# Routing's operations queue behind x's normalisation, turned rows are copied before shifted ones, and the first block's weights are asked for in eight pieces

## The chip, the cores and the metric

The kernel runs on one core of one Trainium2 chip. Its time is the device time of one execution in microseconds (us); a measurement is the median of several. The profile is of one execution, and positions in it are counted from its first instruction.

## What is computed

Sliding-window causal attention over 8 sequences of 576 tokens with 8 heads of 64 features, and behind it a layer of 8 experts in which every token goes to one expert. A local gate decides whether a token takes the expert of its own logits or that of the token before it, so the choice runs as a chain along the sequence.

```python
scores = q @ k.T / sqrt(64)                  # only 0 <= pos_q - pos_k < 64
attn_out = softmax(scores) @ v               # (8, 8, 576, 64) -> x (8, 576, 512)
logits = x @ w_gate                          # 8 experts
local_gate = sigmoid(x @ w_local)
for b in range(B):
    prev_e = -1
    for s in range(S):
        fresh_e = argmax(logits[b, s])
        e = fresh_e if s == 0 or local_gate[b, s] < 0.5 else (prev_e if prev_e >= 0 else fresh_e)
        prev_e = e
        h = maximum(x[b, s] @ w1[e], 0)      # 512 -> 1024
        out[b, s] = softmax(logits[b, s])[e] * (h @ w2[e])
```

## The kernel before

The 4608 tokens are cut into nine stages (`sc`) of 512; in every stage four pairs of heads (`hp`) are worked on, which makes 36 units, written (sc, hp). `attention` runs over the units in this order. For unit i it first issues the scores of unit i + 2 (`scores`: TensorE products, ScalarE exponentials, and on VectorE the multiplication with a mask, L421; for the units in `BIASED`, among them all of stage 6, the mask is added on TensorE instead), then the values of unit i (`values`: 64 small TensorE products, then on VectorE the reciprocal of the sums, L436, for later stages the gate columns, L439, and x's normalisation, L441). The output of the values lies in one of two PSUM buffers (`pair`), used in turns, so the values of a unit wait until the normalisation of the unit two before has read its buffer.

TensorE, ScalarE and SyncE (SP, which issues most DMAs) run in the order of the program (`manual_schedule`). VectorE and GpSimd (POOL) are queues in order too, but a scheduler that works on estimated times puts them together, and it may place an operation that is ready by its estimate ahead of others that the program issues earlier. `issue_after(ins)` adds an order at compile time: what is issued under it on the engine of `ins` comes behind `ins` in the queue.

Between a stage's first units `shift(sc + 1)` copies the rows of v half a tile further, into `vb` of the next stage: ScalarE does L360, L363 and L367, POOL L361 and L365; two of its parts are taken per unit. For stages 0 to 3 the gate logits come from turned rows: `turn` transposes x on TensorE into one of the two PSUM buffers and ScalarE copies the result out (L305); its second half is done at head pair 0 of the next stage. For the later stages (`GATED`) the gate columns ride along with v; `gates` and `spread` make them, by way of the single PSUM bank of `bank`, and ScalarE copies them out (L346 to L348).

`Router.first` finds, from the logits of the first 3 1/2 stages, which tokens fill the first three expert blocks. It is a generator whose parts are issued between the units by `step`, which runs once ahead of the values of a unit and once behind them. Every call takes 0.8 (`HALF`) off `pause`; once `pause` is not above zero the next part is issued, and `pause` becomes its weight plus what was left (not below -0.8). A part is yielded with its weight and with whether the part behind it begins with a PSUM operation; such a part isn't issued in a step called with `free` false. `free` is false at the first step of head pair 3 and at the second of head pair 2 when the next stage is in `GATED`. The parts are `gate` (maxima, two transposes with scans on VectorE behind them, L812 and L822, the carry, L833, the experts, L845, counts, L858, ranks), then `experts_of` and the places (`pl`, `places`), then `table`: comparisons that make one-hot rows (`rowh`, L957) and columns, a product of these (L980), and from it the row indices (`idx1`, `gx1`, L984 to L989). With `gx1` POOL gathers the first block's rows (`Experts.rows`, L1162). `weigh` stores the routing weights.

Two steps are marked in SP's queue for the first block's weights: at unit (6, 3) w1 and at (7, 1) w2 are asked for, each in four pieces of 512 KB at once, behind a tiny DMA (`until`) that makes SP wait for that unit's reciprocals. Then come the expert blocks (`Experts.run`): the first turns its gathered rows on TensorE (L1196, copied by ScalarE, L1197), computes `hidden` (L1414) and, on the way, VectorE's sums of w2 (L1231). SP's next weights wait for gathered rows of the second block (`held`). A second pass of the router (`Router.second`) is interleaved with the first blocks.

Of the kernel before, what the change touches and what calls it, by code (L numbers as in the profile page):

```python
# [8 lines left out]
F32 = mybir.dt.float32  # L9
# [10 lines left out]
P = 128  # L20
# [147 lines left out]
def attention(ctx, tc, ring, kq, v3, v4, vt, vh, xs, lt, ok, wg, wg2, ident, rt, ex):  # L168
# [65 lines left out]

    late = cp.tile([1, 4], F32, name="late")

# [187 lines left out]
    def values(sc, hp, p, x, g):  # L424
        va, vb, n = vas[sc], vbs[sc], width(sc)
        xo = pair()
        for s in range(4):
            for j in range(2):
                for par, w in enumerate((vb, va)):
                    b = 2 * s + par  # L430
                    nc.tensor.matmul(xo[par * WIN:(par + 1) * WIN, j, s * VW:s * VW + n],  # L431
                                     lhsT=p[:, j, b * WIN:(b + 1) * WIN], rhs=w[:, s, 2 * hp + j, :n],
                                     start=True, stop=True)
        o = xo[:, :, :4 * VW].rearrange("p j (c x) -> p j c x", x=VW)
        r = allr[:, sc, hp]
        nc.vector.reciprocal(r, o[:, :, :, DH])  # L436
# [4 lines left out]
        nc.vector.tensor_tensor(x[:, :, hp].rearrange("p c j d -> p j c d"), o[:, :, :, :DH],  # L441
                                rr.to_broadcast([P, 2, 4, DH]), op=Alu.mult)

# [27 lines left out]
    for i, (sc, hp) in enumerate(units):  # L471
# [230 lines left out]
class Router:  # L702
# [9 lines left out]
    def __init__(self, ctx, tc, lt, xs, tabs, ident):  # L712
        self.nc, self.lt, self.xs, self.tabs, self.ident = tc.nc, lt, xs, tabs, ident
        self.pool = ctx.enter_context(tc.tile_pool(name="rt", bufs=1))
        self.tc, self.behind, self.links = tc, None, []
# [58 lines left out]
    def gate(self, part, psum):  # L774
# [170 lines left out]
    def table(self, psum, cs, ns, lo, hi, idx, gx):  # L945
# [5 lines left out]
        for k in range(0, len(pieces), 2):  # L951
            built = []
            for b, m in pieces[k:k + 2]:
                rowh = self.oh_p.tile([P, PIECE, P], BF16, name="rowh")[:, :m]
                if ns == FIRST:
                    sh = [P, m, P]
                    vec.tensor_tensor(rowh, self.io128.to_broadcast(sh), last(lo[:, b:b + m]).to_broadcast(sh),  # L957
                                      op=Alu.is_equal)
                    yield 0.15 * m, False
                one = self.oh_p.tile([P, PIECE, ns], BF16, name="one")[:, :m]  # L960
# [33 lines left out]
    def first(self, psum):  # L994
# [20 lines left out]
        vec.tensor_tensor(pl, rank, mid(self.lim1).to_broadcast(CE), op=Alu.is_ge)  # L1015
        vec.scalar_tensor_tensor(pl, pl, float(2 * N), rank, Alu.mult, Alu.add)
        yield 1.2, False
        vec.tensor_tensor(pl, pl, mid(foff).to_broadcast(CE), op=Alu.add)
        vec.tensor_tensor(pl, pl, self.oh[:, :C1], op=Alu.mult)
        lo, hi = self.places(pl, C1)  # L1020

        vec.tensor_tensor(rank, rank, mid(self.lim1).to_broadcast(CE), op=Alu.subtract)
        yield 2.5, False
        self.weigh(0)
        yield from self.table(psum, slice(0, C1), FIRST, lo, hi, tabs["idx1"], tabs["gx1"])

    def second(self, psum):
# [72 lines left out]
        vec.tensor_tensor(pl, pl, plh, op=Alu.add)  # L1100
        vec.tensor_scalar(none, self.rank[:, :C1], 0.0, float(2 * N), Alu.is_lt, Alu.mult)
        vec.tensor_tensor(pl[:, :C1], pl[:, :C1], none, op=Alu.add)
# [28 lines left out]
class Experts:  # L1131
# [38 lines left out]
    def weights(self, st, n, names=("w1", "w2"), behind=lambda: None):  # L1170
        ej, at = (self.tabs["ej1"], -1 - n) if n < 0 else (self.tabs["ej"], n)
        e = self.nc.values_load(ej[0:1, at:at + 1], engines=[ET.SP], min_val=0, max_val=E - 1,
                                skip_runtime_bounds_check_because="a count of experts, at most E - 1")
        behind()
        for name, w, a, b in (("w1", self.w1, DK, F), ("w2", self.w2, FK, D)):
            if name not in names:
# [6 lines left out]
            st[name] = t.rearrange("p (a b) -> p a b", a=a)  # L1183
        return st

    def begin(self):
# [432 lines left out]
```

## Time and profile before

| | |
|---|---|
| median of 3 runs | 642.59 us (640.96 to 642.63) |
| the profiled execution, its own time | 642.1 us |
| its span, first to last instruction | 640.0 us |
| mean granted TensorE clock | 0.994 |
| instructions | 14994 |
| attention stage, to the first block's matmuls | 0 to 133.4 us |
| HBM traffic | 259 GB/s over the span |

How such a profile is read: PE is TensorE (PEld its weight loads, which overlap), DVE VectorE, ACT ScalarE, POOL GpSimd, SP SyncE's DMA queue. A row of the timeline has start, duration, engine, line, operation, output and inputs, and in brackets how long the engine sat idle before it and what released it. A row of waits has engine, tile and line, the releaser, and the total, number and longest of the waits. "issue" is time for which the profile shows no wait. An engine's idle time matters only where that engine sets the end.

### The profile page before, as it was taken

What the parts mean: (1) busy time and instruction counts of PE and PEld (TensorE: products, weight loads), DVE (VectorE), ACT (ScalarE), POOL (GpSimd) and SP (SyncE); (2) the same over time, 40 slices, a digit from 0 to 9 for tenths busy, and PEclk for the clock granted to TensorE, in tenths of its full rate; (3) what the DMA queues carried; (4) which work ended last, traced back from release to release, by engine and by line L of the source; (5) the groups of instructions that cost most, each with busy time, mean ns of one, the idle gap of its engine ahead of it and who ended that gap; (6) DMA issues with size and microseconds to landing.
All of it is one profiled execution on the core that took longest, in us unless ns stands there. A gap on an engine that the chain in (4) does not pass through costs nothing. (4 is left out here: it accounts for less than half of the span.)

```text
span 640.0 us, 14994 instructions
## 1 busy us (share of the span) xinstructions
PE 615.6 (96%) x6367; PEld 544.2 (85%) x6367; DVE 402.3 (63%) x752; ACT 200.6 (31%) x368; POOL 133.1 (21%) x132
## 2 busy tenths in 40 slices
PE   8889998899999999999999999999999999999995
PEld 7777777788889999978997999887997998899994
DVE  6676588879968775273654683362917752886730
ACT  3766765612572122113120312021211221213120
POOL 5422112430103202120302120211312022111101
PEclk9999998999999999999999999999999999999998
DMA  9999996969757645786958665769768556956501
GB/s 338 416 418 406 385 366 241 348 236 337 237 171 246 244 166 198 242 316 236 387 189 291 218 234 212 259 235 367 263 228 324 185 199 232 379 167 225 209 17 38
DMA packets 29318, 166.43 MB, mean 260 GB/s; under 512 B 8451, under 2 KB 9497, under 8 KB 20026
## 3 DMA queue, kind: packets, MB, share of 16 engines
q1 hardware_dynamic: 20394, 135.54, 58.4%
q0 software_dynamic: 8848, 29.85, 12.2%
q8 instruction: 52, 0.85, 0.5%
q14 instruction: 24, 0.20, 0.1%
HBM read 146.18 MB, written 19.59 MB: 259 GB/s over the span
## 5 line engine op out<-in xcount | busy, mean ns | idle before, releaser
L1394 POOL DMA_INDIRECT out_dram<-y,idx x36 | 41.1, 1141 | 339.1 <-DVE y L1327 196.5
L1318 PE MATMUL hp<-ws,hs 128*128 128x256 f32 x384 | 88.7, 380 | 0.0
L1318 PEld LDWEIGHTS hp<-ws,hs 128*128 128x128 f32 x384 | 72.6, 190 | 10.5 <-issue 0.8
L1268 PE MATMUL hp<-xs,ws 128*128 128x128 f32 x672 | 79.6, 275 | 0.0
L1268 PEld LDWEIGHTS hp<-xs,ws 128*128 128x128 f32 x672 | 77.3, 192 | 0.0
L1327 DVE SCALAR_TENSOR_TENSOR y<-hp,xg,kept 128x256 f32<-128x256 f32 x48 | 22.6, 482 | 74.2 <-issue 47.0
L1414 PE MATMUL hp<-xt,w 128*64 128x64 f32 (+2 forms) x640 | 66.2, 276 | 0.0
L1414 PEld LDWEIGHTS hp<-xt,w 128*128 128x128 f32 (+1 forms) x640 | 60.8, 170 | 4.1 <-issue 0.7
L1318 PE MATMUL hp<-w,h 128*128 128x256 f32 x256 | 61.1, 382 | 0.0
L1162 POOL DMA_INDIRECT xg<-xs,gx x40 | 50.3, 1258 | 45.6 <-issue 37.4
L1279 DVE TENSOR_TENSOR h<-hp,keep 128x512 f32<-128x512 f32 x42 | 28.6, 690 | 48.1 <-PE hp L1268 48.0
L1268 PEld LDWEIGHTS hp<-xt,w 128*128 128x128 f32 x448 | 53.2, 192 | 2.7 <-issue 1.3
L1268 PE MATMUL hp<-xt,w 128*128 128x128 f32 x448 | 54.7, 275 | 0.0
L1318 PEld LDWEIGHTS hp<-w,h 128*128 128x128 f32 x256 | 47.2, 190 | 6.3 <-issue 0.4
L431 PE MATMUL xo<-vb,p 128*64 128x74 f32 (+1 forms) x576 | 44.5, 230 | 7.0 <-issue 2.9
L416 ACT ACTIVATE p<-sp 128x512 f32<-128x512 f32 x72 | 39.2, 595 | 38.0 <-PE sp L385 35.9
L385 PEld LDWEIGHTS sp<-w 64*64 64x64 f32 x1296 | 38.7, 138 | 12.1 <-issue 8.5
L421 DVE TENSOR_TENSOR p<-p,mask 128x1024 f32<-128x1024 f32 x29 | 36.1, 1245 | 19.5 <-ACT p L416 19.3
L431 PEld LDWEIGHTS xo<-vb,p 128*64 128x64 f32 x576 | 38.9, 138 | 9.9 <-issue 4.4
L385 PE MATMUL sp<-w 64*64 64x128 f32 (+1 forms) x1296 | 43.8, 270 | 2.6 <-issue 1.5
L431 PE MATMUL xo<-va,p 128*64 128x74 f32 (+1 forms) x576 | 44.5, 230 | 1.2 <-issue 1.2
L1280 ACT ACTIVATE h<-h 128x512 f32<-128x512 f32 x42 | 26.3, 630 | 59.1 <-DVE h L1279 59.1
(280 smaller groups left out, 955.0 us busy)
## 6 DMA issues: line engine op xcount, KB each, us to landing
w<-in_w_dram SPq DMA_DIRECT2D x42, 2048.0 KB, 9.2
w<-in_kq_dram SPq DMA_DIRECT2D x17, 1024.0 KB, 8.7
w<-in_w_dram SPq DMA_DIRECT2D x24, 512.0 KB, 9.3
xs<-x POOLq DMA_DIRECT2D x9, 1024.0 KB, 9.5
va<-in_v_dram SPq DMA_DIRECT2D x5, 1184.0 KB, 8.9
vtt<-in_vt_dram SPq DMA_DIRECT2D x5, 1024.0 KB, 7.2
va<-in_v_dram SPq DMA_DIRECT2D x3, 1040.0 KB, 12.2
va<-in_v_dram SPq DMA_DIRECT2D x2, 520.0 KB, 6.8
```

The source lines that it names most:

```text
L385: nc.tensor.matmul(sp[j][c * WIN:(c + 1) * WIN, a:b], lhsT=kt[h, hp, block * WIN:(block + 1) * WIN], rhs=qt[h, hp, a:b], start=not biased, ...
L416: nc.scalar.activation(p[:, j], sp[j], Act.Exp, scale=DH ** -0.5)
L421: masked.append(nc.vector.tensor_tensor(p, p, m.to_broadcast([P, 2, SC]), op=Alu.mult))
L431: nc.tensor.matmul(xo[par * WIN:(par + 1) * WIN, j, s * VW:s * VW + n], lhsT=p[:, j, b * WIN:(b + 1) * WIN], rhs=w[:, s, 2 * hp + j, :n], ...
L1162: asked = self.nc.gpsimd.indirect_dma_start(out=x, out_offset=None, in_=self.xs[:rows, :], in_offset=bass.IndirectOffsetOnAxis(ap=gx[:, s: ...
L1268: nc.tensor.matmul(out[:, m, :], lhsT=a[:, kk, m * P:(m + 1) * P], rhs=b[:, kk, :], start=start and m + kk == 0, stop=stop and (m, kk) == ...
L1279: nc.vector.tensor_tensor(o, x, y, op=add)
L1280: nc.scalar.activation(o, x if y is None else o, Act.Relu)
L1318: nc.tensor.matmul(out, lhsT=a[:, m, :], rhs=b[:, m, :], start=start and m == 0, stop=stop and m == FK // 2 - 1, skip_group_check=True)
L1327: nc.vector.scalar_tensor_tensor(y[i][:, j * w:(j + 1) * w], x, pw[i], y2, Alu.mult, Alu.add)
L1394: self.nc.gpsimd.indirect_dma_start(out=self.out[:, :], out_offset=bass.IndirectOffsetOnAxis(ap=st["idx"][:, s:s + 1], axis=0), in_=y, in_ ...
L1414: nc.tensor.matmul(hp[a, i, :], lhsT=st["w1"][:, kk, m * P:(m + 1) * P][:, a], rhs=st["xt"][:, kk, :n], start=(kk == 0), stop=(kk == DK - 1))
```

## The change

- `Router.after()` gives an `issue_after` on x's last issued normalisation (`rt.norm`, set in `values`). Under it are now issued: the rows `rowh` of the first table, which are also made in halves of five chunks with a part each; `experts_of`, the steps of `pl`, `places` and the rank's subtraction in `first`, cut into three parts in place of two; and in `second` the operation that makes `none`.
- The part with the scans in `gate` has the weight 2.4 in place of 1.5 in the first pass.
- The second step of a unit is not free at head pairs 2 and 3 (before: 2 alone) when the next stage is in `GATED`.
- At head pair 0 of stages 1 to 4 the two parts of `shift` are issued behind `turn`, not ahead of it.
- w1 of the first block is asked for in single pieces at (6, 3), (7, 0), (7, 1) and (7, 2), w2 at (8, 0) to (8, 3), each behind its own `until`.

```diff
-    late = cp.tile([1, 4], F32, name="late")
+    late = cp.tile([1, 3 + 2 * HP], F32, name="late")
...
-        nc.vector.tensor_tensor(x[:, :, hp].rearrange("p c j d -> p j c d"), o[:, :, :, :DH],
-                                rr.to_broadcast([P, 2, 4, DH]), op=Alu.mult)
+        rt.norm = nc.vector.tensor_tensor(x[:, :, hp].rearrange("p c j d -> p j c d"), o[:, :, :, :DH],
+                                          rr.to_broadcast([P, 2, 4, DH]), op=Alu.mult)
...
-        for _ in range(2 if sc else 4):
-            next(moves, None) if moves else None
+        late_moves = hp == 0 and sc and sc - 1 not in GATED
+
+        def move():
+            for _ in range(2 if sc else 4):
+                next(moves, None) if moves else None
+
+        if not late_moves:
+            move()
...
+        if late_moves:
+            move()
...
-            ex.jobs = [ex.weights({}, -1, ("w1",), lambda: until(2, allr[:1, sc, hp, 0, :1]))]
+            ex.jobs = [ex.weights({}, -1, (), lambda: until(2, allr[:1, sc, hp, 0, :1]))]
+            ex.piece(ex.jobs[0], "w1", 0)
...
-        step(not (hp == 2 and sc + 1 in GATED))
-        if (sc, hp) == (NSC - 2, 1):
-            ex.weights(ex.jobs[0], -1, ("w2",), lambda: until(3, allr[:1, sc, hp, 0, :1]))
+        step(not (hp >= 2 and sc + 1 in GATED))
+        at = i - (len(units) - 2 * HP)
+        if 0 <= at < 2 * HP and at != HP - 1:
+            until(3 + at, allr[:1, sc, hp, 0, :1])
+            ex.piece(ex.jobs[0], "w1" if at < HP else "w2", at % HP + (at < HP))
...
+    def after(self):
+
+        return self.tc.issue_after(self.norm.ins) if self.norm else nullcontext()
...
-        yield 1.5, True
+        yield 1.5 if part else 2.4, True
...
-                    vec.tensor_tensor(rowh, self.io128.to_broadcast(sh), last(lo[:, b:b + m]).to_broadcast(sh),
-                                      op=Alu.is_equal)
-                    yield 0.15 * m, False
+                    for c in range(0, m, PIECE // 2):
+                        d = min(c + PIECE // 2, m)
+                        sh = [P, d - c, P]
+                        with self.after():
+                            vec.tensor_tensor(rowh[:, c:d], self.io128.to_broadcast(sh),
+                                              last(lo[:, b + c:b + d]).to_broadcast(sh), op=Alu.is_equal)
+                        yield 0.15 * (d - c), False
...
-        self.experts_of(tabs["ej1"], FB, [(FB, fend)])
...
+        with self.after():
+            self.experts_of(tabs["ej1"], FB, [(FB, fend)])
+            vec.tensor_tensor(pl, rank, mid(self.lim1).to_broadcast(CE), op=Alu.is_ge)
+            vec.scalar_tensor_tensor(pl, pl, float(2 * N), rank, Alu.mult, Alu.add)
         yield 1.2, False
...
+        with self.after():
+            vec.tensor_tensor(pl, pl, mid(foff).to_broadcast(CE), op=Alu.add)
+            vec.tensor_tensor(pl, pl, self.oh[:, :C1], op=Alu.mult)
+        yield 0.8, False
+        with self.after():
+            lo, hi = self.places(pl, C1)
+            vec.tensor_tensor(rank, rank, mid(self.lim1).to_broadcast(CE), op=Alu.subtract)
+        yield 1.7, False
...
+        with self.after():
+            vec.tensor_scalar(none, self.rank[:, :C1], 0.0, float(2 * N), Alu.is_lt, Alu.mult)
...
+    def piece(self, st, name, i):
+        w, a, b = (self.w1, DK, F) if name == "w1" else (self.w2, FK, D)
+        if not i:
+            t = self.ring.tile([P, a * b], F32, name="w")
+            st[name] = t.rearrange("p (a b) -> p a b", a=a)
+        m = a // PARTS
+        src = w[bass.ds(st["e"], 1)].rearrange("o p (a b) -> (o p) a b", a=a)
+        self.nc.sync.dma_start(out=st[name][:, i * m:(i + 1) * m], in_=src[:, i * m:(i + 1) * m])
```

More of the change, by code (lines that the diff above doesn't have):

```diff
@@ L714, in __init__ @@
         self.pool = ctx.enter_context(tc.tile_pool(name="rt", bufs=1))
-        self.tc, self.behind, self.links = tc, None, []
+        self.tc, self.behind, self.links, self.norm = tc, None, [], None
         self.rows_of(ctx, tc, "rt_oh1")
@@ L1014, in first @@
         rank = self.rank[:, :C1]
-        vec.tensor_tensor(pl, rank, mid(self.lim1).to_broadcast(CE), op=Alu.is_ge)
-        vec.scalar_tensor_tensor(pl, pl, float(2 * N), rank, Alu.mult, Alu.add)
+        with self.after():
+            self.experts_of(tabs["ej1"], FB, [(FB, fend)])
+            vec.tensor_tensor(pl, rank, mid(self.lim1).to_broadcast(CE), op=Alu.is_ge)
+            vec.scalar_tensor_tensor(pl, pl, float(2 * N), rank, Alu.mult, Alu.add)
         yield 1.2, False
[L1018 to L1023, printed above, removed]
+        with self.after():
[6 more added lines that the diff above has]
+        yield 1.7, False
         self.weigh(0)
@@ L1100, in second @@
         vec.tensor_tensor(pl, pl, plh, op=Alu.add)
-        vec.tensor_scalar(none, self.rank[:, :C1], 0.0, float(2 * N), Alu.is_lt, Alu.mult)
+        with self.after():
+            vec.tensor_scalar(none, self.rank[:, :C1], 0.0, float(2 * N), Alu.is_lt, Alu.mult)
         vec.tensor_tensor(pl[:, :C1], pl[:, :C1], none, op=Alu.add)
@@ L1174, in weights @@
         behind()
+        st["e"] = e
         for name, w, a, b in (("w1", self.w1, DK, F), ("w2", self.w2, FK, D)):
```

## The prediction, made before the result was known

> **What bounds the kernel now.** I read the engine shares first, then TensorE's own waits, then the stretches around those waits.
>
> ```profile
> span 640.0 us, 14994 instructions
> PE 615.6 (96%) x6367; PEld 544.2 (85%) x6367; DVE 402.3 (63%) x752; ACT 200.6 (31%) x368; POOL 133.1 (21%) x132
> 133.41:626.00 492.59, 491.31 (x3487) 440.95 (x3486) 305.34 (x513) 119.38 (x231) 90.69 (x77) 1.00 0.66 239
> ```
>
> TensorE (PE) is the bound. From 133.41 us, where the first expert block's matmuls begin, to 626 us it idles 1.3 us in 492.6. So the experts are a fixed length behind one point, the start of that block, and only what brings this point forward counts. All removable idle time lies in the attention stage ahead of it. Its waits from 40 us on:
>
> ```profile
> PE xo L431 <- issue: 3.4, 3, 1.8
> PE xo L431 <- DVE x L441: 2.5, 1, 2.5
> PE xo L431 <- ACT p L305: 1.5, 3, 0.8
> PE r L822 <- DVE loc L817: 0.9, 1, 0.9
> PE r L812 <- ACT va L348: 0.6, 1, 0.6
> ```
>
> The second row is the largest single wait: unit (6,1), written (stage, head pair), needs the PSUM buffer that x's normalisation of unit (5,3) has to read out.
>
> ```profile
> 96.28 1.24 DVE L1019 TENSOR_TENSOR pl<-pl,oh 128x112 f32<-128x112 f32 x1
> 97.44 1.18 DVE L1101 TENSOR_SCALAR none<-rank 128x112 f32<-128x112 f32 x1
> 99.66 1.49 DVE L957 TENSOR_TENSOR rowh<-io,lo 128x1280 bf16<-128x1280 f32 x1
> 101.06 0.20 DVE L436 RECIPROCAL allr<-xo 128x8 f32<-128x8 f32 x1
> 101.45 0.68 DVE L441 TENSOR_TENSOR x<-xo,allr 128x512 f32<-128x512 f32 x1
> ```
>
> VectorE (DVE) is a queue in order, and routing operations that the program issues three units later were put ahead of that reciprocal. The wait also costs clock (columns: the stretch, its length, busy time of PE, PEld, DVE, ACT and POOL with counts, granted clock, DMA share, GB/s):
>
> ```profile
> 99.67:102.18 2.51, 0.00 (x0) 0.00 (x0) 2.51 (x7) 2.20 (x4) 0.00 (x0) 1.00 0.65 255
> 102.18:103.98 1.80, 1.80 (x32) 1.65 (x32) 1.80 (x9) 0.00 (x0) 0.75 (x1) 0.63 0.24 89
> 103.98:105.90 1.92, 1.92 (x39) 1.80 (x37) 1.73 (x6) 0.00 (x0) 0.00 (x0) 0.50 1.01 412
> 109.76:110.95 1.19, 1.19 (x34) 1.11 (x33) 0.52 (x1) 1.17 (x4) 0.00 (x0) 1.00 0.50 213
> 113.18:114.23 1.05, 1.05 (x40) 0.98 (x37) 1.03 (x2) 1.03 (x3) 1.05 (x2) 1.00 0.97 102
> ```
>
> After 2.51 us of idling, one unit's values take 1.80 us where 1.19 is usual, and its scores 1.92 where 1.05 is usual: 0.61 + 0.87 = 1.5 us more.
>
> **The change part by part.**
>
> *Routing behind x's normalisation.* The guarded operations (rowh, places, pl, none) can no longer run ahead of the last normalisation issued. The wait of 2.5 us and the slow clock of 1.5 us go: -4.0. In its place nothing is late: with DVE free, (5,3) is normalised while PE does the next scores, 1.05 us or more.
>
> *New weights of the parts and the stricter free.* With 2.4 in place of 1.5, and no PSUM part at the second step of head pair 3, L812 moves from (4,3) to the first step of (5,0) and L822 from there to (5,1). Their waits of 0.6 and 0.9 on the same rows have a unit more to pass: -1.5.
>
> *Turned rows first.* At head pair 0 of stages 2 to 4, the copy L305 leaves ahead of L360 and L363:
>
> ```profile
> 55.04 0.63 ACT L360 COPY vb<-va 64x520 f32<-64x520 f32 x1
> 55.57 1.17 ACT L363 COPY vb<-va 64x1184 f32<-64x1184 f32 x1
> 56.76 1.01 ACT L305 COPY p<-xo 128x1024 f32<-128x1024 f32 x1
> 57.83 0.27 PE L431 MATMUL xo<-vb,p 128*64 128x65 f32 x1 [0.82 <-ACT p L305]
> ```
>
> L305 then ends at about 56.05, ahead of PE, which was ready 0.82 before 57.83. ScalarE's sum of the three copies is unchanged, so the next exponentials start as before; vb is read four units later, so the two delayed copies cost nothing. All three waits go: -1.5. POOL's copies of the same shift keep their order.
>
> Together -7.0, all of it ahead of 107.21 us, where the values of (6,2) end.
>
> *What the steps now do to DVE.* Counting the pause by hand (0.8 off per step, a part's weight added) gives the units in which routing is issued (a: the step ahead of the values, b: behind them):
>
> ```
>           L812  L822  L833  L845  L858  pl    places  rowh  L980
> before    4,3b  5,0a  5,0b  5,1b  5,2a  6,0b  6,1a    6,2b  7,1a
> after     5,0a  5,1a  5,1b  6,0a  6,0b  6,3a  7,0a    7,1a  8,0a
> ```
>
> So L812, issued in 5,0a, leaves a pause of -0.8 + 2.4 = 1.6; it is 0.8 in 5,0b and zero in 5,1a, where L822 goes. Of before, the trace has L980 just ahead of the values of (7,1), at 114.66:
>
> ```profile
> L980 PE MATMUL r<-colh,rowh x14: 168/168/181, 114.2 to 114.6; 128*128 128x12 bf16 x14
> ```
>
> After, L845 finds pause above zero in 5,2a, and then no PSUM part may go until 6,0a. All behind it comes later, L980 by three units, in (8,0). That is DVE's heavy stage. The units of stage 6 take their masks as biases on PE; from (7,0) on each has a mask on DVE again:
>
> ```profile
> 116.75 1.22 DVE L421 TENSOR_TENSOR p<-p,mask 128x1024 f32<-128x1024 f32 x1
> 117.88 0.20 DVE L436 RECIPROCAL allr<-xo 128x8 f32<-128x8 f32 x1
> 118.86 1.22 DVE L421 TENSOR_TENSOR p<-p,mask 128x1024 f32<-128x1024 f32 x1
> ```
>
> From start to start that is 1.1 for a mask and 1.0 for a normalisation. The budget from 107.21 to the first block:
>
> ```profile
> 107.21:124.72 17.51, 16.32 (x415) 13.18 (x415) 14.60 (x31) 11.15 (x21) 6.79 (x5) 1.00 0.89 288
> 124.72:133.41 8.69, 6.94 (x179) 6.37 (x173) 6.17 (x13) 3.24 (x6) 0.81 (x1) 1.00 0.89 347
> ```
>
> PE is busy 23.3 of 26.2 us, DVE 14.60 + 6.17 = 20.8. What moves in is read off the stretches that it fills now:
>
> ```profile
> 94.79:96.28 1.49, 1.49 (x48) 1.33 (x52) 1.42 (x12) 1.44 (x4) 0.14 (x1) 1.00 0.99 335
> 98.54:101.06 2.52, 1.13 (x42) 0.97 (x34) 2.36 (x9) 2.50 (x4) 0.01 (x1) 1.00 0.96 367
> 102.62:103.59 0.97, 0.97 (x23) 0.97 (x21) 0.97 (x5) 0.00 (x0) 0.56 (x1) 0.51 0.10 29
> ```
>
> 1.42 + 2.36 + 0.97, and 0.27 for L1019 without its wait: 5.0 us (a few small operations in these rows stay, a few outside them come; I let them cancel). L1019 itself shows one more cost. It took 1.24 where L1022, of the same size, takes 0.27:
>
> ```profile
> 96.09 0.27 DVE L1022 TENSOR_TENSOR rank<-rank,lim 128x112 f32<-128x112 f32 x1
> 96.14 1.26 POOL L361 COPY vb<-va 64x1184 f32<-64x1184 f32 x1 [11.48 <-PE xo L431]
> ```
>
> It ends as POOL's copy does. Stage 7's two POOL copies now meet the moved operations: nothing at best, 2 x 0.97 at worst; I take 0.65, as DVE reaches them midway. The Trainium skill ("SBUF — State Buffer", Who interferes with whom) speaks against the change here: a DVE operation with two SBUF inputs blocks until a reading GpSimd operation ends. By that rule alone both copies would stop one operation each, and the sum would be 1.3 us worse.
>
> DVE therefore becomes the bound of the last nine units. The last values, (8,3), need the normalisation of (8,1), not that of (8,2): 20.8 - 1.0 + 5.0 + 0.65 + about 1.0 in which it waits for exponentials = 26.4 us after 107.21 (in this scale), then 1.2 of values: 27.6 against 26.2 before.
>
> *The gather of the first block's rows.* gx comes behind L980. DVE's work up to it is 14.60 + 5.0 + 0.65 + 1.0, and 0.65 for stage 7's reduction: 21.9. Then POOL issues two gathers:
>
> ```profile
> 117.12 1.79 POOL L1162 DMA_INDIRECT xg<-xs,gx  x1 [2.62 <-DVE gx L989]
> 136.94 1.02 POOL L1162 DMA_INDIRECT xg<-xs,gx  x1 [1.26 <-ACT pa L795]
> DMA to landing us min/median/max: 3.7/4.4/8.3
> 131.94 1.07 ACT L1197 COPY xt<-tp 128x512 f32<-128x512 f32 x2 [3.76 <-issue]
> ```
>
> The second is asked for about 1.8 after gx (0.3, and 1.0 to 1.8 for the first): 23.7. Landing took 8.3 with the weights' queue full and 3.7 without. The pieces leave it part full, so I take 6.0: 29.7. Four transposes (0.55) and one copy (0.54) later, 30.8, the block starts, against 26.2. Before, PE's waits show none on these rows. This wait takes 4.6 of the 7.0 back; ends 28.5 (3.7) and 33.1 (8.3).
>
> *Weights in eight pieces.* w1 is asked for a unit apart from (6,3), w2 over (8,0) to (8,3). SP waits for each unit's reciprocal; behind it stand only the routing weights' store and later the next blocks' weights, which wait for rows gathered after attention. When is w2 wanted, and how long are pieces on their way?
>
> ```profile
> 140.27 1.19 DVE L1231 TENSOR_TENSOR ws<-w 128x1024 f32<-128x1024 f32 x1
> DMA to landing us min/median/max: 9.9/11.8/13.7
> ```
>
> DVE takes its first half 6.9 us after the block's start of 133.41, so at 37.7, and the second some 3 us later. The first half, asked by about 24, is there at 37.7 even at 13.7, w2's slowest landing now; the last piece, asked at 28, comes at 38 to 42. So it costs nothing on the path, or 1 us at worst. The fetch stalls in this stretch (1.19 and 1.75, within "issue") may go, but lie under DVE's wait anyhow.
>
> *Sum.* 7.0 - 4.6 = 2.4 less than the profiled execution's 642.1: 639.7. That run lay 0.5 under the median of 642.6, so 640.2.
>
> **The rivals.**
>
> *DVE keeps up.* If routing still finds room in stage 6, nothing is given back and the fetch stalls go too: 642.6 - 7.0 = 635.6, at best 632.7. For it: PE and DVE both have idle time there now. Against it: 20.8 + 5.0 fill 25.8 of the 19.2 us that this would leave. Chance 0.12.
>
> *The gather is late and the clock falls: slower.* Both POOL copies in the way (23.2), the slow issue (25.3) and 8.3 to land give 33.6, and a start at 34.7: 8.5 lost. PE has then idled about 6 us, and after 2.51 it lost 1.5. With the 7.0 that is 3.0 slower: 645.6. It decides once the second tile lands later than 26.2 + 7.0 - 1.1 = 32.1 after the values of (6,2). Against it: six gathers had a median of 4.4. Chance 0.13.
>
> *The half clock stays.* If the clock fell for another reason than the wait, 1.5 of the gain isn't had: 641.7. For it: the stalls of 1.75 and 1.19 left the clock at 1.00. Against it: no other wait of 2.5 us is in this stage, and none other shows a low clock. The Trainium skill ("TensorE: Matmul & The Clock Gate", What's actually happening) has the clock halve after an idle window of some 3.4 us, more than was idle here. Chance 0.10.
>
> *Nothing comes of it.* The queue orders other routing ahead, or each wait is followed by the next: 642.6. Chance 0.10.
>
> **How the numbers follow.** The forecast has 0.55. About 0.3% (1.9 us, so 640.7 to 644.5) is what a measurement of this kernel can tell from no change. Of the forecast's spread, 637.9 to 642.5, some 0.36 is faster and 0.19 the same; DVE keeping up adds 0.12 to faster; the half clock 0.02 and 0.08; nothing 0.08 same and 0.02 slower; the late gather 0.03 same and 0.10 slower. Faster 0.50, same 0.38, slower 0.12. The range of 635.5 to 643.5 takes in the ends of landing and of the POOL contention and leaves out about 0.1 on each side.
>
> **What would show it.** In the new profile: no wait on x L441 near 100 us and clock 1.00 there; no wait on L305 from 40 us on; L812 and L822 without waits; DVE busy nearly throughout stage 7, with PE waiting for L441 or masks by tenths; L980 just ahead of the values of (8,0); and PE waiting for xg at the first transposes. If PE runs through to the first block, or xg has landed before attention ends, the forecast is too high; if the wait there exceeds 5 us or the clock falls, it is too low.

## The result and the profile after

The changed kernel is slower: 647.34 us (median of 6 runs, 645.73 to 648.89) against 642.62 for the kernel before on the same chip (6 runs, 640.96 to 643.95), a ratio of 1.0061 with a 95% interval of 1.0041 to 1.0082. The forecast was 640.2. Ratios here and below are worked out from the fast runs alone, so they can differ a little from the quotient of the two medians.

First the head of the page after, then TensorE's own waits from 40 us to 146 us, the rows that answer to the five shown of before (engine, tile and line, releaser, total, number, longest):

```profile
span 645.9 us, 15007 instructions
PE 619.1 (96%) x6367; PEld 546.1 (85%) x6367; DVE 400.1 (62%) x753; ACT 200.8 (31%) x368; POOL 130.5 (20%) x132
```

```profile
PE tp L1228 <- DMA xg<-xs,gx: 4.5, 2, 3.0
PE xo L431 <- issue: 2.8, 3, 1.5
PE xo L431 <- DVE x L441: 2.4, 2, 2.2
PE sp L385 <- issue: 2.3, 3, 1.4
PE r L848 <- DVE allr L436: 0.5, 1, 0.5
```

The three waits on L305 and the two in the scans (now L827 and L837) are gone. A wait on x's normalisation of 2.2 us is back under the same name, but it is another one: it stands at 126 us, in the last stage, not at 100. The first row is new: TensorE turns the first block's gathered rows and they are not there.

The stretches of after, cut where the prediction cut them, from the end of the values of (6,2) to the first block's matmuls and from there on (columns: stretch, length, busy time of PE, PEld, DVE, ACT and POOL with counts, granted clock, DMA share, GB/s):

```profile
105.94:138.46 32.52, 25.28 (x587) 20.91 (x587) 23.41 (x66) 14.50 (x27) 7.61 (x6) 0.88 0.72 232
138.46:626.00 487.54, 486.25 (x3444) 436.55 (x3443) 304.19 (x511) 119.04 (x230) 87.73 (x76) 1.00 0.67 242
```

With the rows of before this splits the 5.9 us between the two spans exactly. The values of (6,2) end 1.27 earlier (105.94 against 107.21), the stretch to the first block is 6.32 longer (32.52 against 26.20), and what follows is 0.85 longer (507.44 to the span's end against 506.59). Ahead of (6,2) little was won; behind it much was lost.

**Where it was lost.** The product of the table stands in the lists of operations as follows, before first and after second (start of the first and end of the last of 14; its line is L980 before and L999 after):

```profile
L980 PE MATMUL r<-colh,rowh x14: 168/168/181, 114.2 to 114.6; 128*128 128x12 bf16 x14
```

```profile
L999 PE MATMUL r<-colh,rowh x14: 168/168/182, 121.8 to 122.6; 128*128 128x12 bf16 x14
```

It is just ahead of the values of (8,0), as the count of the pause had it. VectorE's timeline behind it (start, duration, operation), of which I leave out the small steps between the copy of the product and gx:

```profile
122.36 1.22 DVE L421 TENSOR_TENSOR p<-p,mask 128x1024 f32<-128x1024 f32 x1
...
123.88 0.68 DVE L441 TENSOR_TENSOR x<-xo,allr 128x512 f32<-128x512 f32 x1
124.48 0.66 DVE L545 TENSOR_REDUCE lt<-g 128x36 f32<-128x288 f32 x1
125.06 0.16 DVE L1001 COPY t<-r 128x12 f32<-128x12 f32 x1
...
125.94 0.17 DVE L1008 TENSOR_SCALAR gx<-at 128x6 uint32<-128x6 f32 x1
126.02 1.22 DVE L421 TENSOR_TENSOR p<-p,mask 128x1024 f32<-128x1024 f32 x1
```

The product ends at 122.6, but VectorE reads it at 125.06, behind a mask, the normalisation of (7,3) and that stage's reduction: VectorE runs some 3 us behind, since the values of (7,3) ended at 120.9. Then POOL gathers (timeline; in brackets the idle time and its releaser):

```profile
126.39 1.78 POOL L1184 DMA_INDIRECT xg<-xs,gx  x1 [0.78 <-DVE gx L1008]
128.48 1.75 POOL L1184 DMA_INDIRECT xg<-xs,gx  x1 [0.31 <-issue]
```

The landing of the two, and TensorE's stretches, the first of them from ahead of the gather (columns as above):

```profile
DMA to landing us min/median/max: 6.1/6.4/6.7
```

```profile
119.60:126.18 6.58, 6.30 (x183) 5.73 (x182) 6.41 (x20) 3.86 (x9) 0.75 (x1) 1.00 0.64 176
126.18:128.36 2.18, 0.00 (x0) 0.03 (x1) 2.15 (x5) 0.00 (x0) 1.78 (x1) 1.00 1.01 376
129.62:132.61 2.99, 0.00 (x0) 0.03 (x1) 1.66 (x5) 0.00 (x0) 0.61 (x1) 0.70 0.85 291
133.70:135.24 1.54, 0.00 (x1) 0.00 (x1) 0.00 (x0) 0.58 (x1) 0.00 (x0) 0.50 0.97 341
136.28:138.46 2.18, 2.18 (x34) 2.03 (x33) 0.00 (x0) 0.58 (x1) 0.00 (x0) 0.50 0.03 13
138.46:145.16 6.70, 6.70 (x28) 5.67 (x27) 4.81 (x19) 0.95 (x2) 3.38 (x4) 0.81 0.69 228
```

VectorE is busy 6.41 of 6.58 us up to there. TensorE then idles 2.18 us for the normalisation of (8,0), works 1.26, idles 2.99 for the first gathered tile, turns it in 1.09 and idles 1.54 for the second. From about 131 the clock is 0.50. Behind the transposes come, in TensorE's queue, the values of (8,3): at half clock they take 2.18 where 1.19 is usual. Only then does the first block start, itself at a clock of 0.81 in its first 6.7 us.

**Where the removed waits went.** An ordinary table shows it: the end of the last product of each unit's values in the timeline, after minus before in us. A fall is a gain made in that unit, a rise is a loss.

| end of unit | (3,0) | (3,1) | (3,3) | (4,1) | (4,3) | (5,0) | (5,2) | (5,3) | (6,0) | (6,1) | (6,2) |
|---|---|---|---|---|---|---|---|---|---|---|---|
| after minus before | +0.35 | -0.54 | +0.35 | -0.27 | +0.17 | -1.77 | -1.98 | -0.96 | +0.47 | -2.09 | -1.27 |

The waits on L305 go at (3,1) and (4,1), those of the scans at (5,0), that on the normalisation at (6,1); from (3,0) on the falls add up to some 6 us. But each is followed by a rise, some 4.6 us together, mostly where TensorE stands still with no releaser: from 38 us to the end of (6,2) the stalls of this kind over 0.25 us add up to 5.1 us in six places, against 1.6 in two before. Two of them in the timeline after:

```profile
98.51 0.28 PE L431 MATMUL xo<-vb,p 128*64 128x74 f32 x1 [1.00 <-issue]
105.00 0.22 PE L431 MATMUL xo<-va,p 128*64 128x74 f32 x1 [1.47 <-issue]
```

Before has no stall over 0.3 us at either place.

### The profile page after: what moved, and what is told of

Its sections match the earlier page's. It is cut to its first block, busy times and chain, and to the rows that moved or that the text cites. A ratio compares the mean times of both kernels' runs of the same rounds, so it can differ in the third digit from the quotient of the medians.

```text
span 645.9 us, 15007 instructions
## 1 busy us (share of the span) xinstructions
PE 619.1 (96%) x6367; PEld 546.1 (85%) x6367; DVE 400.1 (62%) x753; ACT 200.8 (31%) x368; POOL 130.5 (20%) x132
## 5 line engine op out<-in xcount | busy, mean ns | idle before, releaser
L1184 POOL DMA_INDIRECT xg<-xs,gx x40 | 48.8, 1221 | 43.5 <-issue 37.1
```

The costliest lines, as they stand in the source:

```text
L1184: asked = self.nc.gpsimd.indirect_dma_start(out=x, out_offset=None, in_=self.xs[:rows, :], in_offset=bass.IndirectOffsetOnAxis(ap=gx[:, s: ...
```

## The experiments

Two theories stood against each other. *Late table*: the new weight and the stricter `free` put the table into (8,0), and the gather with what follows it costs more than the removed waits bring. *Queue rule*: what is queued behind the normalisation is late or makes VectorE the bound. Beside them: is each removed wait really won?

### The parts alone

The four parts, each put alone into the kernel before. All four ran beside the same runs of before (642.84).

**Queueing alone** (`after()` around `rowh`, `experts_of`, `pl`, `places` and `none`):

```diff
+        with self.after():
+            self.experts_of(tabs["ej1"], FB, [(FB, fend)])
+            vec.tensor_tensor(pl, rank, mid(self.lim1).to_broadcast(CE), op=Alu.is_ge)
...
+                    with self.after():
+                        vec.tensor_tensor(rowh, self.io128.to_broadcast(sh), last(lo[:, b:b + m]).to_broadcast(sh),
+                                          op=Alu.is_equal)
```

> Before, with the queueing behind x's normalisation alone (rowh whole, old weights of the parts, old order of copies, weights in four and four pieces). Three theories stand. LATE TABLE: the loss comes from the step timetable, which puts the table's matmuls into unit (8,0); here they stay in (7,1), so PE waits nowhere for the gathered rows, and the wait of 2.5 us on x L441 near 100 us with its half clock goes: 1.5 to 4 us faster, 638.5 to 641. QUEUE RULE: the loss comes from DVE's operations held behind normalisations; then this is slower, 644 or more, with PE waiting on L441 or on rowh. FETCH: each wait that goes is followed by a stall without releaser, about every 165 matmuls; the gain is under 2 us and such stalls of 0.5 to 1.5 us appear between 85 and 110 us.

642.9 us, ratio 0.9989 (0.9966 to 1.0012): no difference. The wait on L441 near 100 us is gone, and this stands in its place, in the timeline and then in the stretches of this kernel:

```profile
101.55 0.28 PE L431 MATMUL xo<-vb,p 128*64 128x74 f32 x1 [2.38 <-issue]
```

```profile
99.18:101.55 2.37, 0.00 (x0) 0.00 (x1) 0.00 (x0) 1.89 (x3) 0.93 (x2) 1.00 0.84 307
103.00:105.00 2.00, 2.00 (x38) 1.88 (x32) 1.87 (x12) 0.93 (x2) 0.00 (x0) 0.50 1.01 408
```

VectorE did nothing in the first stretch (its column is 0.00), so TensorE wasn't waiting for it. 2.51 us of waiting became 2.37 us of a stall, and the clock fell behind it just as before. The queue rule as a cause of loss falls, and with it the hope of a gain from this part alone. What TensorE waits for here is told below, with the stalls without a releaser.

**Turned rows first, alone:**

```diff
+        late_moves = hp == 0 and sc and sc - 1 not in GATED
...
+        if late_moves:
+            move()
```

> Before, with only the turned rows' copy ahead of the shifted copies. If nothing follows the waits, the 1.5 us on L305 go and the time is 641.1. FETCH: the stalls without releaser between 20 and 65 us grow or new ones appear, and under 0.5 us is left, 642.1 to 642.6. LATE TABLE and QUEUE RULE say nothing of it; neither expects it slower.

643.18 us, ratio 1.0001 (0.9981 to 1.0021). The waits on L305 from 40 us on are gone, and nothing of it is left at the end: at (3,1) this kernel is 0.57 ahead of before, at (3,3) 0.05 behind it.

**Eight pieces alone** (`piece` and the eight `until`):

```diff
+        at = i - (len(units) - 2 * HP)
+        if 0 <= at < 2 * HP and at != HP - 1:
+            until(3 + at, allr[:1, sc, hp, 0, :1])
+            ex.piece(ex.jobs[0], "w1" if at < HP else "w2", at % HP + (at < HP))
```

> Before, with only the first block's weights asked for in eight pieces. FETCH: the stalls of 1.2 and 1.75 us near 121 and 127 us, which fall into a time of full DMA queues, shrink to under 0.5 each, and the gathered rows land in 4 to 6 us instead of 8: 1.5 to 2.9 us faster, 639.7 to 641. If the eight pieces were the loss instead (w2 asked too late), the first block or its sums of w2 would wait and the time be 644 or more. LATE TABLE expects no wait on the gathered rows here.

641.43 us, ratio 0.9978 (0.9955 to 1.0001): at best a little faster. The stall of 1.19 us near 121 that before shows is gone, the later one is still there with 1.48.

**The pace alone** (weight 2.4 and the stricter `free`):

```diff
-        yield 1.5, True
+        yield 1.5 if part else 2.4, True
...
-        step(not (hp == 2 and sc + 1 in GATED))
+        step(not (hp >= 2 and sc + 1 in GATED))
```

> Before, with only the weight of 2.4 and the stricter free steps: the table's matmuls move to (8,0), all else is as before. LATE TABLE: PE waits for the gathered rows ahead of the first block, 4 us or more, the clock halves, and the time is 645 to 649, as much as the whole change or more, as the weights' queue is full (8 us to land). QUEUE RULE and FETCH: within 1.5 us of before.

650.95 us, ratio 1.0116 (1.0093 to 1.0139). This small part alone makes the kernel slower than the whole change does. Its row of waits, the product of the table, and the stretches of the wait and of the values of (8,3) behind it:

```profile
PE tp L1196 <- DMA xg<-xs,gx: 6.9, 2, 6.6
```

```profile
L980 PE MATMUL r<-colh,rowh x14: 168/168/181, 126.3 to 126.6; 128*128 128x12 bf16 x14
```

```profile
132.40:139.06 6.66, 0.02 (x2) 0.03 (x1) 1.26 (x4) 0.00 (x0) 1.29 (x2) 0.86 0.89 355
141.44:143.61 2.17, 2.17 (x34) 2.02 (x33) 0.00 (x0) 0.59 (x1) 0.00 (x0) 0.50 0.00 0
```

The same chain as in the changed kernel, without any queueing behind the normalisation: late table, a wait of 6.66 us, half clock, values of 2.17 us.

### The pace undone

**The whole change but for the two lines of the pace:**

```diff
-        yield 1.5 if part else 2.4, True
+        yield 1.5, True
...
-        step(not (hp >= 2 and sc + 1 in GATED))
+        step(not (hp == 2 and sc + 1 in GATED))
```

> The changed kernel with the old weight of 1.5 and the old free steps: queueing, copies and eight pieces stay, the table's matmuls go back to (7,1). LATE TABLE: the waits on the gathered rows (4.5 us) and the half clock behind them go, and the time is 5 us or more under the changed kernel: 639 to 642.5, by as much under before as the stalls without releaser leave of 7 us. QUEUE RULE: it stays at 645 or more.

639.21 us against 643.74 for before beside it, ratio 0.9928 (0.9904 to 0.9951): this kernel beats both. Its table, then the stretch from the end of (6,2) to the first block:

```profile
L999 PE MATMUL r<-colh,rowh x14: 167/168/181, 112.5 to 112.8; 128*128 128x12 bf16 x14
```

```profile
105.50:128.46 22.96, 22.96 (x586) 19.51 (x585) 21.65 (x46) 14.41 (x27) 7.62 (x6) 1.00 0.87 283
```

With the table back at its old place TensorE doesn't idle at all between (6,2) and the first block, 22.96 of 22.96 us; before it was 23.26 of 26.20. Its span, 635.3, is 10.6 less than the changed kernel's, and 9.56 of this lies in that stretch (32.52 against 22.96). So the two lines cost 10.6 us between these two profiles; by the ratios (1.0061 and 0.9928) it is some 8.6. The rest of the change brings 4.7 against the span of before. Only 1.7 of that is there at the end of (6,2), at 105.50; 3.2 come behind it, where before lost 1.19 and 1.75 us in two stalls without a releaser; 0.3 is lost again in the blocks. What is left of waits from 40 us to 146 us:

```profile
PE xo L431 <- issue: 2.4, 2, 1.6
PE sp L385 <- issue: 1.9, 3, 1.4
PE r L837 <- DVE loc L832: 0.9, 1, 0.9
```

**The same without the queueing.** Before, with the turned rows first and the eight pieces, but neither the queueing nor the pace. On record ahead of it stood 639 to 640 if copies and pieces bring the gain alone, and 641 to 642, with the wait of 2.5 us and the half clock behind it still there, if the queueing is needed. It took 643.17 us, ratio 0.9977 (0.9954 to 0.9999), against 645.1 for before beside it. By these two ratios the queueing, which alone brought nothing, is needed for most of the 0.7%. The wait is still there:

```profile
PE xo L431 <- DVE x L441: 2.9, 2, 2.5
```

But the clock stayed at 1.00 from 99 to 106 us, so the half clock doesn't always come with this wait.

**Which of the two lines?** The weight kept and the old `free`, then the stricter `free` kept and the old weight (before beside them: 645.1):

```diff
-        step(not (hp >= 2 and sc + 1 in GATED))
+        step(not (hp == 2 and sc + 1 in GATED))
```

> The changed kernel with the old `free`, the weight 2.4 kept. By the count of the pause the table's product goes ahead of the values of (7,3), or just behind them, instead of (8,0): one unit earlier than changed, two later than in the kernel with both undone. Late-table theory: the second gathered tile lands about 2 us earlier than in the changed kernel; TensorE's wait for xg falls from 4.5 to about 2 us or less, no half clock at the first block, time between 639.2 and 647.3: about 642 to 644, ratio to before 0.998 to 1.002. Rival (what counts is DVE's load in the last stage, not where the table is): no better than the changed kernel, 647, ratio 1.006.

650.12 us, ratio 1.0100 (1.0047 to 1.0154). That is no better than the changed kernel, where I had expected about the time of before. The row of its table says why:

```profile
L999 PE MATMUL r<-colh,rowh x14: 167/168/168, 122.2 to 122.5; 128*128 128x12 bf16 x14
```

The product is issued right behind the values of (7,3), half a unit earlier by the order, but TensorE gets there at 122.2, no earlier than in the changed kernel (121.8): its values of (7,3) come 0.85 later, and it waits 0.5 us for the PSUM bank. Its first gather starts at 126.04 (changed: 126.39). So this run doesn't vary what it was to vary, and doesn't decide between the two theories; it only agrees that a table just as late is no faster.

```diff
-        yield 1.5 if part else 2.4, True
+        yield 1.5, True
```

> The changed kernel with the old weight of 1.5, the stricter `free` kept. By the count of the pause the table's product is in (8,0), where the changed kernel has it, though L822 to L858 come up to a unit earlier. Late-table theory: as late as the changed kernel, a wait for xg of 4 us or more with the clock at one half behind it, 645 to 648, ratio about 1.006. Rival (the later scans of the weight 2.4 are what costs): near the kernel with both undone, 639 to 641, ratio 0.993 to 0.997.

652.79 us, ratio 1.0123 (1.0081 to 1.0166): slower than the 645 to 648 expected, with the table at 124.8, 3 us later than in the changed kernel, and this row of waits:

```profile
PE tp L1228 <- DMA xg<-xs,gx: 4.5, 2, 3.5
```

Either line by itself puts the table into the last stage. In the six kernels with such a table (the changed one and the runs with the pace, without the pieces, with the transposes last, with one of the two lines) the first block starts 15.4 to 17.3 us after the table's product.

### The end of attention

**Transposes behind the values of (8,3).** The changed kernel, with the first block's transposes queued behind the last values, so that TensorE needn't stand in front of them:

```diff
-        self.turn(jobs[0], True)
+        with tc.issue_after(rt.final.ins) if hasattr(rt, "final") else nullcontext():
+            self.turn(jobs[0], True)
```

> The changed kernel with the transposes of the gathered rows queued behind the values of (8,3) on PE. The rows come as late as in the changed kernel, but the values fill some of the wait. If the order of PE's queue is the part that I left out, the last values (2.2 us at half clock) leave the path: 1 to 2.5 us faster than the changed kernel, 645 to 646.5, still slower than before. If only the landing of the rows counts, no difference: 647.

649.57 us, ratio 1.0085 (1.0061 to 1.0109). The gain that I expected didn't come. The wait for the gathered rows shrinks to 2.0 us and the block starts at 137.22, 1.24 earlier than in the changed kernel, but the clock:

```profile
125.78:127.93 2.15, 0.00 (x0) 0.03 (x1) 2.12 (x5) 0.00 (x0) 1.78 (x1) 1.00 1.01 385
127.93:132.29 4.36, 3.59 (x64) 3.18 (x64) 2.88 (x7) 0.00 (x0) 1.75 (x1) 0.62 0.91 273
137.22:142.70 5.48, 5.48 (x13) 4.41 (x14) 1.47 (x8) 0.33 (x1) 3.40 (x4) 0.51 0.96 354
```

It falls at 128.96, a microsecond behind the idle 2.15 us, and stays at one half till 142.6, so the block's first matmuls run at 0.51. In the changed kernel it is back at 141. Here the order that puts work into the wait for data didn't help: the work ran at half clock, and the second tile came no sooner (135.43 against 135.24).

**The changed kernel with its weights in four and four pieces:**

```diff
-            ex.piece(ex.jobs[0], "w1", 0)
...
+        if (sc, hp) == (NSC - 2, 1):
+            ex.weights(ex.jobs[0], -1, ("w2",), lambda: until(3, allr[:1, sc, hp, 0, :1]))
```

> The changed kernel with w1 and w2 asked for in four and four pieces as before, all else changed. LATE TABLE with a full queue: w2 is then asked for at (7,1) and its rest competes with the gather; the rows land in 6 to 8 us instead of 6.1 and 6.7, and stalls without releaser near 121 and 127 us come back: 0 to 3 us slower than the changed kernel, 647 to 650. If the eight pieces were a part of the loss: faster than 646.

649.97 us, ratio 1.0104 (1.0069 to 1.0139), with a wait of 6.0 us for xg and the block at 140.29. The pieces aren't what makes the change slower; the intervals of this run and of the changed kernel overlap, so that they help is likely, not shown.

### The stalls without a releaser

**Fewer loads.** The kernel with the old pace, with the queries and keys of stages 6 to 8 not loaded (stage 5's are used again, so it computes something else). If full DMA queues were behind the stalls, they should shrink.

```diff
+            elif sc > 5:
+                kqs[sc], kts[sc], qts[sc] = kqs[5], kts[5], qts[5]
```

> The kernel of the run before last but two (old weights and steps, queueing, copies, eight pieces), with the queries and keys of stages 6 to 8 not loaded (stage 5's are used again, so the results of these stages are other ones): 6 MB less for the DMA queues between 57 and 100 us, PE's work the same. FETCH from full queues: the stalls without releaser from 60 to 110 us shrink to under 0.3 each, 1.5 to 4 us less up to 105 us than in the kernel that loads them; those before 55 us stay. If the stalls have nothing to do with the queues, they stay as long.

638.42 us, ratio 0.9918 (0.9893 to 0.9943); the kernel with the old pace has 0.9928. The stall near 103 us is there with its full size in both; first the row with all loads, then without:

```profile
104.52 0.22 PE L431 MATMUL xo<-va,p 128*64 128x74 f32 x1 [1.61 <-issue]
```

```profile
104.02 0.28 PE L433 MATMUL xo<-va,p 128*64 128x74 f32 x1 [1.62 <-issue]
```

The DMA share just ahead of it, 96 to 102 us, was high in both (0.94 and 0.96), so for this stall the run doesn't decide. From 60 to 64 us the share fell from 1.03 to 0.34, and yet the kernel lost 0.67 us against before from (3,1) to (3,3), where the one with the old pace lost 0.89; but of neither loss more than 0.3 us is in stalls of this kind.

**A shifted count.** Over all kernels I had noticed that these stalls come after nearly the same numbers of TensorE's matmul records, at regular distances. So the kernel with the old pace got 60 more warming transposes at its start:

```diff
-    warm(12)
+    warm(72)
```

> The kernel with both pace parts undone, with 72 warming transposes of the identity at the start in place of 12: 60 more at 0.235 us, so about 14 us more of time, or 650 to 654. What it is for is where TensorE's stalls without a releaser come. In the kernel with both pace parts undone they come after about 498, 665, 833, 1005, 1338, 1671 and 2824 matmul records. If they are tied to the count of instructions (as loading instructions in blocks would be): after the same counts, so at places some 60 matmuls earlier in the program; the stall of 1.4 us ahead of scores at record 1005 and that of 1.6 us within values at 2824 leave their places. If they are waits of these places that the profile doesn't resolve (a buffer, a queue): at the same lines and places, so after counts higher by 60 (558, 725, 893, 1065), or gone where the loads have 14 us more of a lead.

650.35 us in a single run (before: 646.14), inside the 650 to 654 expected. The counts in the expectation are too high, and so is the distance of 165 in that of the queueing alone. Counted from the start with each record once they are lower, as these stretches show, which end inside a stall of the old pace's kernel and of this one (TensorE's busy time and records alone):

```profile
0.00:40.20 40.20, 33.23 (x730) 1.00 0.97 383
0.00:43.45 43.45, 37.77 (x731) 1.00 0.87 335
```

All the stalls without a releaser over 0.25 us up to the first block, as the number of PE records ahead of each:

| warming transposes | | | | | | | | | |
|---|---|---|---|---|---|---|---|---|---|
| 12 | 349 | 476 | 604 | 730 | | 985 | 1240 | | 2131 |
| 72 | | 476 | 604 | 731 | 858 | 986 | | 1877 | 2386 |

The distances are multiples of some 127 records. The counts stay, so the places in the program move by 60 records. (A unit's values are 32 records in these traces, not 64.) The stall at 730, within the scores issued in unit (2,0), left its place; at 731 there is now one within the values of (1,3), just ahead of them. The two rows:

```profile
40.25 0.27 PE L385 MATMUL sp<-w 64*64 64x64 f32 x2 [1.36 <-issue]
```

```profile
43.49 0.27 PE L431 MATMUL xo<-va,p 128*64 128x65 f32 x1 [0.79 <-issue]
```

So these stalls belong to the count of TensorE's instructions, not to a buffer or a queue at that place.

**What TensorE waits for.** The DMA packets of the kept traces show it. One of the queues is called instruction; it moves 52 packets of 16 KB in a run. In the run with the queueing alone, the stretch from 99.1 to 100.2 us has one of them (number, MB, share of the time of 16 engines):

```profile
q8 instruction: 1, 0.02, 5.5%
```

It starts at 99.17, as TensorE stops, takes about 0.97 us (5.5% of 16 times 1.1) and has landed at 100.12; TensorE goes on at 101.55, 1.43 later. It is so everywhere: in the fourteen traces, all 107 stalls without a releaser over 0.25 us ahead of 150 us end 1.2 to 1.6 us behind the landing of such a packet, and their counts differ by multiples of some 127 records. So TensorE most likely stands there for want of instructions, which come in blocks. The link is one of time alone, but it holds in every case.

What makes a stall long is when the packet comes and when TensorE gets there. At record 2131 the changed kernel was there at 103.53, the kernel before only at 106.33; the packet landed at 103.73 and at 103.01. So the first stalled and the second didn't. At record 2004 the queueing alone made the packet itself late (100.12 against 95.98 before). Why a packet comes when it does wasn't found.

## Why the prediction was wrong

- **The bound.** Right: TensorE idles 1.29 us of the 487.5 from the first block to 626, and the block's start sets the end but for 0.85 us of half clock.
- **Removed waits, -7.0.** This is the first step that failed. The waits went where the prediction said, but "in its place nothing is late" was not so. Only 1.27 of the 7.0 was there at the end of (6,2). Of the rest, 3.5 us went into stalls without a releaser, in which TensorE most likely waits for its instructions (5.1 us from 38 us on in place of 1.6): it came sooner to places where the packet came no sooner, or even later. A row for it was in the profile of before: "issue", 3.4 us in three stalls, stood at the head of the very view from which the waits were read, and I booked nothing for it ahead of (6,2). Of the remaining 2.2 us, 0.3 was lost ahead of 38 us and 0.5 in a new wait (L848, for the reciprocals); the rest wasn't split further. The rival "nothing comes of it ... each wait is followed by the next" described this part and had 0.10.
- **The half clock, 1.5 of it.** Right in its place: after shows no low clock near 100 us. But the run with the queueing alone shows the clock fall behind a stall of 2.37 us just as behind the wait, so the clock follows idling, whatever causes it. And with the pieces alone, and with pieces and copies without the queueing, the wait of 2.5 us stood and the clock stayed at 1.00: that before lost 1.5 us there was partly chance (see the clock rule below).
- **Turned rows first, -1.5.** The waits went, the gain did not stay (0.05 behind before at (3,3) with this part alone).
- **Weights of the parts and the stricter free, -1.5.** The timetable was right: the product comes ahead of (8,0). But I booked the two lines as a gain of 1.5 with a cost of 4.6 behind it, when they were the whole loss: 10.6 us between the spans with and without them, some 8.6 by the ratios.
- **The gather.** Of this term one half was right. Predicted: gx 21.9 after (6,2), rows landed at 29.7. Measured: the first gather starts at 126.39, and TensorE goes on with the second tile at 135.24, which is 29.3 after 105.94. gx came 1.7 sooner than forecast; the second gather was asked for 2.4 behind it in place of 1.8, and its landing took 6.7 us in place of 6.0.
- **From the rows to the block.** This is the second step that failed: 1.1 was booked, 3.2 came (135.24 to 138.46). I counted four transposes and a copy at full speed. Left out were the values of (8,3), which stand behind the transposes in TensorE's queue, and the half clock in which all of it ran. With 0.85 more in the first block, and 0.4 less for the landing, the 4.6 became 7.2.
- **DVE as the bound of the last nine units.** Only in part. With the old pace VectorE was busy 21.65 of 22.96 us and TensorE didn't wait for it once. In the changed kernel it bound from (7,3) on: 6.41 of 6.58 us busy, and 2.15 of the 2.18 that TensorE waits ahead of the values of (8,2). Of the 0.65 for POOL's copies there was 0.37, in one place (timelines of VectorE and POOL, after):

```profile
112.08 0.64 DVE L1039 TENSOR_TENSOR pl<-pl,oh 128x112 f32<-128x112 f32 x1
112.64 0.26 DVE L1043 TENSOR_TENSOR rank<-rank,lim 128x112 f32<-128x112 f32 x1
```

```profile
111.37 1.22 POOL L365 COPY vb<-va 64x1184 f32<-64x1184 f32 x1
```

  The operation ended as the copy did (112.72 and 112.59); it waited for the copy's rest, not for a whole one.
- **Pieces at no cost.** Held; they may even help.
- **The rivals.** "The gather is late and the clock falls" gave 645.6; the span was 645.9 and the median 647.3. Its result came about, but not by its mechanism alone: the second tile landed at 29.3, before the 32.1 that it set as its point. What made it decide was that the 7.0 on the other side were 1.3. "DVE keeps up" at 635.6 comes nearest to the change with the old pace, where TensorE waited for nothing in the last stage: a ratio of 0.9928 to 642.6 gives 638.0.
- **The clock rule.** The Trainium skill ("TensorE: Matmul & The Clock Gate", What's actually happening) has the clock halve after an idle window of some 3.4 us. By the length of the idling alone the runs here don't follow this. The clock fell behind 2.15 us of it (transposes last) and behind 2.37 (queueing alone). With the pace alone it was still 0.97 over the first 5.2 us of a wait that begins at 132.40:

```profile
132.40:137.60 5.20, 0.02 (x1) 0.00 (x0) 1.26 (x4) 0.00 (x0) 1.29 (x2) 0.97 1.02 405
```

  With the pieces alone it fell behind two waits of 0.56 and 0.93 us, and not around the wait of 2.5 that ended at 104.18:

```profile
81.89:85.30 3.41, 1.87 (x46) 1.39 (x46) 3.03 (x8) 1.80 (x5) 2.98 (x3) 1.00 0.98 375
85.30:88.71 3.41, 3.41 (x61) 3.05 (x63) 2.74 (x9) 1.54 (x2) 0.00 (x0) 0.50 0.99 374
102.37:105.78 3.41, 1.60 (x50) 1.52 (x54) 3.41 (x12) 1.52 (x3) 0.75 (x1) 1.00 0.13 49
```

  The low stretches of the attention stage are 3.41 us long or whole multiples of it: 102.63 to 106.05 before, 137.25 to 144.08 with the pace alone, 130.79 to 141.03 in the changed kernel, 128.96 to 142.62 with the transposes last. So the clock is set in steps of 3.41 us, and what a wait of 2 or 3 us costs depends on how it lies to them: the wait of before lay in one step, 99.22 to 102.63, and left 0.90 us of work in it; with the pieces alone it was spread over two, with 2.70 and 1.60 us of work. How little work makes the clock fall stays open: 1.87 us of 3.41 was little enough once, and 1.60 another time was not.

## What to carry to other kernels

Before a wait is booked as a gain, look for what TensorE meets next at the earlier time, and count stalls without a releaser as such a thing: here they took back half of the 7.0 us. When an edit changes the rhythm of interleaved work, follow its last product to the consumer that stands first in the next phase; here 0.9 more in one weight and one stricter condition moved it by three units. And measure the parts of a change one by one: here two lines turned a gain of 0.7% into a loss of 0.6%.

## What the hardware showed that was not expected

- TensorE stalled after fixed counts of its matmul records, which differ by multiples of some 127, for 0.3 to 2.6 us, and kept to the count when 60 transposes were put ahead (476, 604, 731 against 476, 604, 730). Each of the 107 stalls ended 1.2 to 1.6 us behind the landing of a 16 KB packet of the instruction queue. The longest of them, 2.61 us, was in the run with the added transposes, at 99.26 us.
- The clock was halved for 3.41 us or whole multiples of it, and a wait of 2.5 us cost it in one kernel and not in another.
- The half clock outlasts its cause: in the run with the transposes last, 2.15 us of idling were followed by a low clock until 142.6 us (0.62 over the first 4.36 us behind them, 0.51 in the block), though only shorter waits lay in between.
